# Nyström attention with a mixture of experts: quarter loads for the first batch, weight scales built from exponent bits, and a new order of work

## The chip, the cores and the metric

The kernel runs on one core of one Trainium2 chip. The metric is device time in microseconds of one execution, median of several runs; lower is better. The core has five engines that run in parallel, each in the order of its own instruction list: PE (TensorE, matrix products), DVE (VectorE), ACT (ScalarE), POOL (GpSimd) and SP (SyncE, which here only issues transfers). Sixteen DMA engines move data between HBM and the on-chip memory. An instruction waits on semaphores for what it needs, and everything behind it on its engine waits with it.

## The reference

The attention is Nyström's with 32 landmarks per head; its output goes through a mixture of eight experts, each token to the one expert of its highest gate. Shapes are 8 batches x 8 heads x 576 tokens x 64.

```python
m = 32; scale = 1/8
q_lm = q.reshape(B,H,m,18,D).mean(3);  k_lm = k.reshape(B,H,m,18,D).mean(3)
A, Bm, C = sm(q, k_lm), sm(q_lm, k_lm), sm(q_lm, k)      # softmax(scale * a @ b.T)
Z = Bm.T / (norm1(Bm) * norminf(Bm) + 1e-6)
for _ in range(6): Z = 2*Z - Z @ Bm @ Z
x = (A @ Z @ C @ v)                                       # 4608 tokens x 512
logits = xn @ en.T / tau;  e = argmax(logits);  gate = max(softmax(logits))
out[tokens of e] = gate * (relu(x @ w1[e]) @ w2[e])
```

## The kernel before, in words

Work is cut by batch: 576 tokens, all 8 heads, in eight batches. For each batch the attention part makes landmark sums of keys and queries (`sums`), inverts the 32x32 landmark matrix in six steps (`inverse`, `powers`), forms the weighted values (`values`, `weighted`), softmaxes the queries against the landmark keys (`queries`, `scored`: the tile `ab`), and joins the inverse and the weighted values to `wt` (`landmarks`). All tokens of a batch are guessed to go to one expert (`guess`, `choose`); the experts' weights for that guess are loaded (`weights`), and a last step (`mistakes`) counts tokens for which the guess was wrong and would start a general path.

The expert part runs in 16-bit pairs. `first_weights` multiplies the loaded w1 by `wt`, `scaled` writes the product as a high and a low half (`ww`) under a power-of-two scale, and `first` makes `ht = relu(ab @ ww)` from 96 matmuls of 288 columns. `second` makes the output from `ht` and `w2c`, which are scaled halves of w2. The scales come from three sums of squares or absolute values: `bound` (of `wt`), `first_scale` (of w1; for batch 0 one scale for each of its four quarters, "parts") and `second_weights` (of w2). Each sum is added across partitions by a one-column matmul in `total`; `scale_by` masks the exponent, and reciprocals turn it into a factor.

Loads are issued by SP alone, in order: keys and queries of batch 0 in two halves each, the values, batch 1's keys and queries, then weights as soon as a guess is there. `sums` takes each half either as one DVE reduction of 1152 elements a partition, or as an addition of halves on POOL (`half`) with a DVE reduction of 576.

The order is written out. Each step is a generator; the table TURNS names, turn by turn, the generator that goes on, CHOICES says which engine takes a step that several could take, BANKS which PSUM bank, and WARM at which turn how many dummy products of 128 columns PE gets (`keep_warm`, up to four in one matmul of up to 512 columns, line 604; nothing reads them). So the tables fix every engine's instruction list. Outputs leave through three `yt` tiles in turn; SP reads the count of wrong guesses (`misi`) into a register before the last outputs.

Lines that matter below: L648 loads, L682 and L685 sums, L1003 to L1018 `total` and `scale_by`, L1059 to L1066 `bound`, L1348 squares of w1, L1362 and L1364 its factor, L1416 and L1418 the two halves of `ww`, L514 every product, L1572 and L1574 the outputs.

## Time and profile before

| | before |
|---|---|
| median of 3 runs | 403.74 us (400.25, 403.74, 404.1) |
| the profiled execution, whole | 400.08 us |
| its span, first to last instruction | 398.4 us |
| mean granted TensorE clock | 0.998 |
| PE busy | 378.3 us (95%) |
| DVE busy | 317.9 us (80%) |
| ACT busy | 250.9 us (63%) |
| POOL busy | 91.0 us (23%) |
| moved by DMA | 78.78 MB |

The span is followed on one core. A busy engine is one with an instruction in flight, so a short wait that ends while the last product is still draining does not count as idle. The chain of waits goes back from the last instruction to whatever released each step, and so names the engine that set the end.

### The profile page before, as it was taken

How to read it: one execution, taken by the hardware profiler on the slowest of the kernel's cores; microseconds unless marked ns; L12 is line 12 of the kernel's file. 1: busy time of each engine (PE TensorE's matmuls, PEld its weight loads, DVE VectorE, ACT ScalarE, POOL GpSimd, SP SyncE). 2: the span in 40 equal slices, each digit the busy share in tenths (PEclk: the TensorE clock that was granted, in tenths of full speed). 3: DMA queues.
4: the chain of work that ended last, by engine and by line, in shares of the span. 5: the costliest groups of instructions: out<-in, count | busy, mean ns of one | idle time of the engine just before them, and what ended most of it. 6: DMA issues, size and time to landing. Idle time of an engine off the chain costs nothing.

```text
span 398.4 us, 15143 instructions
## 1 busy us (share of the span) xinstructions
PE 378.3 (95%) x6366; PEld 235.1 (59%) x6366; DVE 317.9 (80%) x921; ACT 250.9 (63%) x617; POOL 91.0 (23%) x94
## 2 busy tenths in 40 slices
PE   3789999999999999999999999999999999999993
PEld 1446745676645765567655675467745675478552
DVE  5999998899987989878997899658978886656521
ACT  1369986785688778735988793543786768336200
POOL 5164255301302131302455300102121220000100
PEclk9999999999999999999999999999999999999999
DMA  8997984517684997215993767015672085013012
GB/s 310 379 369 265 395 287 112 231 49 257 191 350 184 294 363 265 97 56 183 396 381 99 239 207 237 28 56 175 217 276 82 28 284 180 34 50 146 2 66 90
DMA packets 22669, 78.78 MB, mean 198 GB/s; under 512 B 2752, under 2 KB 5056, under 8 KB 20800
## 3 DMA queue, kind: packets, MB, share of 16 engines
q1 hardware_dynamic: 22304, 77.54, 54.0%
q8 instruction: 52, 0.85, 0.9%
q14 instruction: 25, 0.20, 0.2%
q10 hardware_dynamic: 288, 0.18, 0.2%
HBM read 62.96 MB, written 14.75 MB: 195 GB/s over the span
## 4 chain that ended last, share of the span: by engine, by line
PE 77%; DVE 11%; ACT 4%; DMA 3%; issue 2%; POOL 0%; SPq 0%; DVEq 0%; ACTq 0%
PE ps L514 75%; DMA wstage<-w 1%; DVE ht L1482 1%; ACT junk L1232 1%; DVE w2c L1472 1%; PE ps L604 1%; DVE cm L824 1%; DMA k_t<-kT 1%; ACT junk L1432 1%; DVE asum L961 1%; DMA out<-yt 1%; ACT ec L861 1%; ACT junk L1348 1%; DVE ww L1418 1%; DVE qsum L685 1%
## 5 line engine op out<-in xcount | busy, mean ns | idle before, releaser
L514 PE MATMUL ps<-w2c,ht 128*128 128x512 f16 (+2 forms) x1176 | 196.8, 340 | 0.0
L514 PEld LDWEIGHTS <-ht 128*128 128x128 f16 (+1 forms) x1176 | 95.2, 102 | 81.7 <-issue 3.2
L514 PE MATMUL ps<-ab,ww 128*128 128x288 f16 x768 | 101.0, 286 | 0.1
L514 PEld LDWEIGHTS <-ww 128*128 128x128 f16 x768 | 72.8, 98 | 24.2 <-issue 2.5
L1480 ACT ACTIVATE ht<-ps 128x288 f16<-128x288 f32 x128 | 48.2, 423 | 27.0 <-PE ps L514 26.3
L1482 DVE SCALAR_TENSOR_TENSOR ht<-ps,ht 128x288 f16<-128x288 f32 x128 | 53.7, 447 | 6.9 <-ACT ht L1480 6.6
L1232 ACT ACTIVATE junk<-ps 128x512 bf16<-128x512 f32 (+1 forms) x40 | 23.8, 595 | 29.0 <-DVE lga L1223 17.6
L1472 DVE SCALAR_TENSOR_TENSOR w2c<-wstage,wsc,w2c 128x1024 f16<-128x1024 f32 x28 | 37.0, 1322 | 2.1 <-ACT w2c L1470 2.0
L1348 ACT ACTIVATE junk<-wstage 128x1024 bf16<-128x1024 f32 x32 | 34.0, 1062 | 5.3 <-DMA wstage<-w 5.0
L972 POOL TENSOR_TENSOR ab<-at,ab 128x576 f16<-128x576 f32 x14 | 17.9, 1283 | 68.5 <-ACT ab L970 68.5
L1250 POOL TENSOR_TENSOR nrm<-ssq,half 128x5 f32<-128x5 f32 x8 | 9.4, 1175 | 97.4 <-ACT junk L1232 97.4
L1470 ACT ACTIVATE w2c<-wstage,wsc 128x1024 f16<-128x1024 f32 x23 | 26.1, 1148 | 4.8 <-PE ps L514 2.5
L1432 ACT ACTIVATE junk<-wstage 128x1024 bf16<-128x1024 f32 x25 | 26.5, 1059 | 2.1 <-DMA wstage<-w 1.7
L1574 ACT ACTIVATE yt<-ps,gfac 128x512 f32<-128x512 f32 (+1 forms) x26 | 15.8, 619 | 18.9 <-PE ps L514 17.8
L861 ACT ACTIVATE ec<-ps,cneg 128x144 f32<-128x144 f32 x64 | 23.4, 388 | 6.1 <-DVE cneg L851 3.5
L682 POOL TENSOR_TENSOR half<-q_t 128x576 f32<-128x576 f32 x13 | 17.9, 1380 | 27.4 <-DMA q_t<-qT 7.5
L1416 ACT ACTIVATE ww<-ps,wsc 128x1024 f16<-128x1024 f32 (+1 forms) x18 | 17.6, 1018 | 10.1 <-PE ps L514 3.6
L981 POOL TENSOR_TENSOR ae<-ae,am 128x576 f32<-128x576 f32 x13 | 17.1, 1315 | 26.9 <-DVE am L955 20.8
L1418 DVE SCALAR_TENSOR_TENSOR ww<-ps,wsc,ww 128x1024 f16<-128x1024 f32 (+1 forms) x18 | 20.6, 1156 | 0.7 <-ACT ww L1416 0.6
L682 POOL TENSOR_TENSOR half<-k_t 128x576 f32<-128x576 f32 x11 | 14.2, 1295 | 26.1 <-DMA k_t<-kT 20.4
L514 PE MATMUL ps<-ek 32*32 32x64 f32 (+1 forms) x768 | 16.0, 214 | 2.4 <-DVE ek L1035 2.1
L981 POOL TENSOR_TENSOR ae<-ae,asum 128x576 f32<-128x576 f32 x9 | 10.4, 1157 | 33.4 <-DVE asum L795 8.3
(220 smaller groups left out, 497.2 us busy)
## 6 DMA issues: line engine op xcount, KB each, us to landing
wstage<-w SPq DMA_DIRECT2D x64, 512.0 KB, 6.3
v<-v SPq DMA_DIRECT2D x16, 640.0 KB, 5.1
k_t<-kT SPq DMA_DIRECT2D x7, 1152.0 KB, 9.4
q_t<-qT SPq DMA_DIRECT2D x7, 1152.0 KB, 8.6
out<-yt SPq DMA_DIRECT2D x31, 256.0 KB, 2.3
abs__140<-ab SPq DMA_DIRECT2D x8, 576.0 KB, 5.4
k_t<-kT SPq DMA_DIRECT2D x2, 576.0 KB, 4.5
q_t<-qT SPq DMA_DIRECT2D x2, 576.0 KB, 6.5
```

The costliest lines, as they stand in the source:

```text
L514: pe.matmul(o, lhsT, rhs, start=start, stop=stop)
L682: pool.tensor_tensor(out=half, in0=sv[:, :, :, 0:9], in1=sv[:, :, :, 9:18], op=ALU.add)
L861: act.activation(ects[g][:, QS * x:QS * x + QS], pc[:, a, c], AF.Exp, bias=neg[:, 4 * g + 2 * a + c:4 * g + 2 * a + c + 1], scale=SCALE / ...
L981: pool.tensor_tensor(out=x, in0=x, in1=z, op=op)
L1232: act.activation(junk[lo:hi, 0:512].rearrange("p (j g x) -> p j g x", j=4, g=2), pfv[lo:hi, :, n, :, 0:D], AF.Square, scale=1.0 / ASCALE, ...
L1348: act.activation(junk, stage[1, b, q], AF.Square, accum_out=sq[:, q:q + 1])
L1418: vec.scalar_tensor_tensor(out=ww[:, 1], in0=pw, scalar=sc, in1=ww[:, 0], op0=ALU.mult, op1=ALU.subtract)
L1432: act.activation(junk, stage[2, b, q], AF.Abs, accum_out=sq[:, q:q + 1])
L1470: act.activation(w[:, 0], st, AF.Copy, scale=sc)
L1472: vec.scalar_tensor_tensor(out=w[:, 1], in0=st, scalar=sc, in1=w[:, 0], op0=ALU.mult, op1=ALU.subtract)
L1480: act.activation(ht[:, 0, r], ph[:, 0:HS], AF.Relu)
L1482: vec.scalar_tensor_tensor(out=ht[:, 1, r], in0=ph[:, 0:HS], scalar=0.0, in1=ht[:, 0, r], op0=ALU.max, op1=ALU.subtract)
```

## The change

Four things are edited, and the tables that fix the order are replaced as a whole.

The keys and queries of batch 0 are loaded in four quarters each, and `sums` reduces each quarter of 576 elements by itself; the new CHOICES give all eight to DVE. The scales are built by integer arithmetic on exponent bits: `root` masks them, and one subtraction from a constant (or from `kw`) gives the reciprocal power of two, where a multiplication and a reciprocal stood. The addition of 1e-30 on DVE ahead of each total is gone: squares now carry a bias tile `tiny` (1e-17) on ACT and write the sum as bf16, and the accumulators of w2's sums are filled with 1e-30 by POOL at the start. `second_weights` takes the reciprocal of its total as it is. WARM asks for 200 dummy products where it asked for 93.

```diff
-TURNS = ("06060633000b33060606003300340b36...        (2050 turns)
+TURNS = ("000606060607060633063333060b060b...
-WARM = {20: 36, 37: 2, 90: 18, 100: 3, 105: 7, 111: 13, 159: 10, 216: 4}
+WARM = {3: 40, 26: 58, 45: 20, 75: 24, 92: 1, 96: 10, 102: 1, 114: 25, 137: 13, 204: 8}
...
+    absw = cst.tile([P, B, 5], F32, name="absw")
+    pool.memset(absw, 1e-30)
+    tiny = cst.tile([P, 1], F32, name="tiny")
+    pool.memset(tiny, 1e-17)
+    part16 = cst.tile([P, P], BF16, name="part16")
+    pool.memset(part16, 2.0 ** -15)
...
-            parts = 1 if b else 2                      # loads
+            parts = 1 if b else 4
-        parts = 2                                      # sums
+        parts = 2 if b else 4
...
-    def total(sq, n):
+    def total(sq, by=ones16):
-        yield V(4)
-        s16 = wst.tile([P, 4], BF16, name="ws16", bufs=3)[:, 0:n]
-        vec.tensor_scalar(s16, sq, 1e-30, None, op0=ALU.add)
         pf, done = yield from take(T(10, 2, cols=4), 1)
-        mm(pf[:, 0:n], ones16, s16)
+        mm(pf[:, 0:1], by, sq)
...
+    def root(f2):
+        hb = wst.tile([P, 1], I32, name="whb", bufs=4)
+        vec.tensor_scalar(hb, f2.bitcast(I32), 1, EXP_MASK, op0=ALU.logical_shift_right, op1=ALU.bitwise_and)
...
-        vec.tensor_scalar(hbw[:, b:b + 1], f2.bitcast(I32), 1, EXP_MASK, ...)         # bound
-        vec.tensor_scalar(invw[:, b:b + 1], hbw[:, b:b + 1].bitcast(F32), 2.0 ** 58, ...)
-        vec.reciprocal(scw[:, b:b + 1], invw[:, b:b + 1])
+        vec.tensor_scalar(kw[:, b:b + 1], hb, -1.0, float(264 << 23), op0=ALU.mult, op1=ALU.add)
+        vec.tensor_scalar(scw[:, b:b + 1].bitcast(I32), hb, -1.0, float(196 << 23), ...)
+        vec.tensor_scalar(invw[:, b:b + 1], hb.bitcast(F32), 2.0 ** 58, ...)
...
-                act.activation(junk, stage[1, b, q], AF.Square, accum_out=sq[:, q:q + 1])     # first_scale
+                act.activation(junk, stage[1, b, q], AF.Square, bias=tiny, accum_out=sq[:, q:q + 1])
-            yield from scale_by(inv, f2, 2.0 ** 59, True)
-            vec.tensor_scalar(sc, hbw[:, b:b + 1].bitcast(F32), 2.0 ** 58, inv, ...)
-            vec.reciprocal(sc, sc)
+            hb = yield from root(f2)
+            vec.tensor_scalar(sc.bitcast(I32), hb, -1.0, kw[:, b:b + 1], op0=ALU.mult, op1=ALU.add)
...
-        yield from scale_by(inv2[:, b:b + 1], f2, 2.0 ** -14, False)                  # second_weights
-        vec.reciprocal(sc, inv2[:, b:b + 1])
+        vec.reciprocal(sc, f2)
-        vec.tensor_scalar(ginv[:, b:b + 1], inv2[:, b:b + 1], inv1[:, b:b + 1], 1.0 / ASCALE, ...)
-        vec.tensor_scalar(ginv[:, b:b + 1], ginv[:, b:b + 1], invw[:, b:b + 1], ...)
+        vec.tensor_scalar(ginv[:, b:b + 1], sc1[:, b:b + 1], sc, ASCALE, ...)
+        vec.reciprocal(ginv[:, b:b + 1], ginv[:, b:b + 1])
```

DVE's list from its first landmark sum on, in the kernel before (`ksum`, `qsum` are the sums, `half` is what POOL has added ahead, `es` belongs to the experts' norms):

```order
L685 TENSOR_REDUCE ksum<-half 128x64
L685 TENSOR_REDUCE ksum<-k_t 128x64
L616 TENSOR_REDUCE es<-ps 128x8
L685 TENSOR_REDUCE qsum<-q_t 128x64 x2
L621 TENSOR_SCALAR er<-er 128x8
L623 RECIPROCAL er<-er 128x8
```

The same place in the changed kernel:

```order
L689 TENSOR_REDUCE ksum<-k_t 128x32 x4
L689 TENSOR_REDUCE qsum<-q_t 128x32
L620 TENSOR_REDUCE es<-ps 128x8
L689 TENSOR_REDUCE qsum<-q_t 128x32 x3
L625 TENSOR_SCALAR er<-er 128x8
L718 TENSOR_REDUCE bm_222<-ps 128x2
```

Four reductions, the first of them behind POOL, have become eight that wait for loads alone; the rows after them are the same work.

DVE's list where one of batch 0's four w1 factors is made, before (`ws` is the added 1e-30, `whb` the masked exponent, `wsc` the factor, `at` and `ws_` are attention work):

```order
L1003 TENSOR_SCALAR ws_593<-wsq 128x1
L967 STREAM_TRANSPOSE at<-ae 128x576
L1014 TENSOR_SCALAR whb<-ps 128x1
L1064 TENSOR_SCALAR invw<-hbw 128x1
L1018 TENSOR_SCALAR inv1h<-whb 128x1
L723 TENSOR_REDUCE bs_625<-be 128x2
L1362 TENSOR_SCALAR wsc_624<-hbw,inv1h 128x1
L1364 RECIPROCAL wsc_624<-wsc_624 128x1
```

And in the changed kernel (`sc1h` is the factor):

```order
L634 RECIPROCAL con<-con 128x1
L971 STREAM_TRANSPOSE at<-ae 128x576
L1012 TENSOR_SCALAR whb<-ps 128x1
L1095 COPY ws__648<-ps 128x128
L1360 TENSOR_SCALAR sc1h<-whb,kw 128x1
L636 TENSOR_SCALAR con<-con 128x1
```

Five rows for a factor have become two. Between DVE's row L623 (L627 in the changed kernel) and its first `ww` row there were 84 rows and are 73.

DVE's last rows, before (`misi` is the count of wrong guesses, `misf` and `mis16` lead to it, `yt` is an output):

```order
L1572 TENSOR_SCALAR yt_7206<-ps_74,gfac_123 128x512
L1572 TENSOR_SCALAR yt_7208<-ps_74,gfac_123 128x256
L1614 CAST misi_145<-ps_74 128x1
L1562 TENSOR_LOAD misi_145
L1572 TENSOR_SCALAR yt_7249<-ps_74,gfac_123 128x256
L1572 TENSOR_SCALAR yt_7254<-ps_74,gfac_123 128x512
```

And in the changed kernel:

```order
L1602 TENSOR_REDUCE misf_7100<-gs_7086 128x1
L1605 CAST mis16_7111<-misf_7100 128x1
L1567 TENSOR_SCALAR yt_7121<-ps_74,gfac_129 128x512
L1567 TENSOR_SCALAR yt_7129<-ps_74,gfac_129 128x512
L1609 CAST misi_150<-ps_74 128x1
L1557 TENSOR_LOAD misi_150
```

The output of 512 columns that was DVE's last instruction now stands ahead of the count, and both halves of the very last output go to ACT. On PE the count's product moves from behind 18 to behind 6 of the last chunk's 48 products of 256 columns.

## Rows read from the trace of the kernel before

**Rows 1.** Busy time by stretch: PE, PEld, DVE, ACT, POOL, then PEclk, DMA share, GB/s.
```profile
0.00:35.00 35.00, 23.60 (x568) 13.28 (x568) 29.77 (x105) 16.32 (x41) 15.56 (x35) 1.00 0.95 358
10.00:35.00 25.00, 20.06 (x560) 11.74 (x558) 24.04 (x91) 15.04 (x40) 10.29 (x11) 1.00 1.00 377
35.00:390.00 355.00, 353.11 (x5787) 220.64 (x5786) 287.40 (x816) 234.09 (x576) 75.45 (x60) 1.00 0.52 184
```

**Rows 2.** The chain that ended last: start us, us, engine and what.
```profile
0.81 4.00 DMA k_t<-kT
...
92.41 0.29 DVE ek L1035
...
160.74 20.05 PE ps L514 x557
```

**Rows 3.** Timeline of the start: start us, us, what, [idle before <- releaser].
```profile
1.73 1.18 SPq L648 DMA_DIRECT2D q_t<-qT  x2
...
6.20 0.75 DVE L685 TENSOR_REDUCE ksum<-half 128x64 f32<-128x576 f32 x1 [2.50 <-POOL half L682]
...
7.08 3.89 PE L604 MATMUL ps<-ones 128*128 128x512 bf16 x9
...
8.26 2.60 DVE L685 TENSOR_REDUCE qsum<-q_t 128x64 f32<-128x1152 f32 x2
...
17.87 1.15 PE L604 MATMUL ps<-ones 128*128 128x512 bf16 x5
```

**Rows 4.** Loads of the first and second query half: KB, us to landing.
```profile
q_t<-qT SPq DMA_DIRECT2D x1, 576.0 KB, 6.0
q_t<-qT SPq DMA_DIRECT2D x1, 576.0 KB, 7.0
```

**Rows 5.** DVE groups from 10 to 36 us: count, busy us, mean ns, idle before.
```profile
L1018 DVE TENSOR_SCALAR inv1h<-whb 128x1 f32<-128x1 f32 x4 | 0.6, 148 | 0.0
L1364 DVE RECIPROCAL wsc<-wsc 128x1 f32<-128x1 f32 x4 | 0.6, 148 | 0.1
L1003 DVE TENSOR_SCALAR ws<-wsq 128x1 bf16<-128x1 f32 x4 | 0.6, 146 | 0.0
```

**Rows 6.** Timeline from 26 to 34 us, the way to the first expert product.
```profile
26.96 0.27 ACT L1087 COPY wt<-ps 128x128 f32<-128x128 f32 x1 [0.45 <-PE ps L514]
...
29.67 0.67 ACT L970 CAST ab<-at 128x576 f16<-128x576 f32 x1 [0.22 <-DVE at L967]
...
30.25 1.05 ACT L1348 ACTIVATE junk<-wstage 128x1024 bf16<-128x1024 f32 x1
...
31.33 1.84 ACT L1416 ACTIVATE ww<-ps,wsc 128x512 f16<-128x512 f32 x3
...
32.67 0.74 DVE L1418 SCALAR_TENSOR_TENSOR ww<-ps,wsc,ww 128x512 f16<-128x512 f32 x1
...
33.06 1.07 PE L514 MATMUL ps<-ab,ww 128*128 128x288 f16 x6
```

**Rows 7.** The page's costliest groups: two ACT passes over 1024 columns.
```profile
L1348 ACT ACTIVATE junk<-wstage 128x1024 bf16<-128x1024 f32 x32 | 34.0, 1062 | 5.3 <-DMA wstage<-w 5.0
L1470 ACT ACTIVATE w2c<-wstage,wsc 128x1024 f16<-128x1024 f32 x23 | 26.1, 1148 | 4.8 <-PE ps L514 2.5
```

**Rows 8.** Timeline: an undisturbed run of second expert products.
```profile
370.62 5.57 PE L514 MATMUL ps<-w2c,ht 128*128 128x512 f16 x25
```

**Rows 9.** PE groups by shape, whole span: all products of that shape.
```profile
L514 PE MATMUL ps<-w2c,ht 128*128 128x512 f16 x744 | 169.1, 379 | 0.0
```

**Rows 10.** Timeline of the end.
```profile
388.17 3.44 PE L514 MATMUL ps<-w2c,ht 128*128 128x256 f16 x30
...
389.18 3.96 SPq L1579 DMA_DIRECT2D out<-yt  x3
...
391.64 0.47 ACT L1574 ACTIVATE yt<-ps,gfac 128x256 f32<-128x256 f32 x1 [15.02 <-PE ps L514]
392.03 0.75 DVE L1572 TENSOR_SCALAR yt<-ps,gfac 128x512 f32<-128x512 f32 x1 [2.27 <-DMA out<-yt]
```

## The prediction

> **What bounds the kernel now.** I read busy time by stretch first, then the chain of waits, then the timeline of the start and of the end. The stretches show three parts [rows 1]. Up to 35 us PE is busy 23.6 us of 35, so 11.4 us of its time are lost; between 10 and 35 us DVE is busy 24.04 of 25 us, so here DVE's list sets the pace. From 35 to 390 us PE is busy 353.1 of 355 us: it is the bound, and only 1.9 us stand open to be seen. After the last product the output drains. The chain says the same: it starts with the first key load, leaves PE at about 92 us, runs over DVE, ACT and one weight load, and is back on PE for good at 160.74 us [rows 2]. The work that PE has to do is not changed by the diff, so I cost what happens before PE is saturated, what happens after its last product, and what can move in between.

> The sum is made against the profiled execution, 400.08 us: 398.4 of span and 1.68 around it. The runs shown scatter by 1% about a median that is 3.66 us above it: 400.25, 403.74 and 404.1. The mean of these three and the profiled one is 402.0, and I put the forecast for a median on that.

> **Landmark sums.** Before, POOL adds the halves of the first load, DVE waits for it until 6.20, and the last sum ends at 8.26 + 2.60 = 10.86 us [rows 3]. The loads are close behind: the first key half is issued at 0.81 and lands 4.00 later, at 4.8 [rows 2]; the first query half lands at 1.73 + 6.0 = 7.7, and the second, issued about half of the 1.18 us later, at about 2.3 + 7.0 = 9.3 [rows 3, 4]. In the changed kernel eight sums of 576 elements run on DVE, 0.75 each (the row of that shape [rows 3]), 6.0 us in all against 4.7. The last quarter lands at about 9.4, as the same bytes are on the way, and its sum ends at 10.2 to 10.3. Gain 0.55 us. Bounds: if the first quarter comes no sooner than the first half does now, 4.8 + 6.0 = 10.8, nothing gained; if DVE could follow the 9.3 at once, 10.05, 0.8 gained.

> **Scales.** On DVE's list between L623 and the first half of `ww` stand 11 rows fewer. Small rows last 0.146 to 0.148 us [rows 5], 1.6 us in all; started in each other's shadow they are worth less, about 0.1 each. I take 1.2 and keep 0.9 and 1.65. By DVE alone the first DVE row of `ww` then moves from 32.67 [rows 6] by 0.55 + 1.2 to 30.9.

> ACT gives a later time. `wt` moves up by the sums and one removed row, 0.7 us, from 26.96 to 26.3. Then come three squares, one cast and the first part of `ww`. From `wt` to the cast, with two squares, ACT takes 29.67 - 26.96 - 0.22 of waiting = 2.49; the third square with its accumulator takes 1.08 (30.25 to 31.33), the cast 0.58 to the next start, a part of `ww` a third of 1.84, 0.61 [rows 6]. New is the bias tile, an operand read per partition. Two passes over 1024 columns differ by one such operand, a scale, and by 1148 - 1062 = 86 ns [rows 7]; no row has a bias tile at this length. With it, 26.3 + 2.49 + 1.08 + 3 x 0.086 + 0.58 + 0.61 = 31.3, when DVE's row can start: 32.67 - 31.3 = 1.35 us sooner. [...] Over the other batches the bias costs ACT 35 x 0.086 = 3.0 us (28 squares of w1 and 7 short ones), while DVE loses six rows in each of seven batches, 6.1 us.

> I take 1.2 us for the start, a little under ACT's 1.35 because every hand-over between the engines must hold; the bounds are 0 and 1.75 (DVE's own limit). The dummies are priced at nothing while PE waits anyway: 11.4 us lost there are their cover [rows 1]. [...]

> **The end.** Now SP sends three outputs only after the count of wrong guesses is there, at 389.18; a tile comes free by that, and DVE writes the last output at 392.03 to 392.78, although PE's last product ends near 391.6 and ACT's copy at 392.11 [rows 10]. In the new list that output is written ahead of the count, and the last instruction is ACT's copy, so the last transfer leaves 392.78 - 392.11 = 0.67 us sooner. I take 0.6; bounds 0 and 0.7.

> **The middle.** It is laid anew and nothing in the diff shortens PE's work there. Visible are 1.9 us of gaps [rows 1]. Short ones hide in the busy time: undisturbed, a product of 512 columns takes 5.57 / 25 = 0.223 us, and 744 of them 165.8; they took 169.1, so 3.3 us are hidden in this shape [rows 8, 9]. DVE's 6.1 us less against ACT's 3.0 more make a small gain likelier than a loss. I take 0.4, and for the range a gain of 4 and a loss of 4.

> **The sum.** 1.2 + 0.6 + 0.4 = 2.2 us. For an execution like the profiled one: 400.08 - 2.2 = 397.9. For the median, on the mean of the four: 402.0 - 2.2 = 399.8.

> **Rivals.**
> A: the new order also closes the gaps of the middle. It would take most of the 1.9 visible and 3.3 hidden us, 4.5 in all: 402.0 - 1.8 - 4.5 = 395.7. For it speaks that the chain is off PE from 92 to 161 us, on the engines that lose work; against it that gaps of both sizes belong to work in a fixed order of dependence, which a new list can only shift.
> [...]
> C, slower: ACT's list puts squares of w1 ahead of exponentials and `ht` copies that DVE and PE wait for. ACT already waits 5.0 us for weights to land [rows 7], hidden now. If the waits come to stand on PE's path and double, 10 - 1.8 = 8.2 us are lost: 410.2. It decides from 5.8 us on, where the loss passes 1%. Against it: DMA share is 0.52 after 35 us [rows 1], so most weights land early.
> D, slower: each smaller load pays its start-up again. The first load took 4.0 us, while the next ones followed at about 1.55 us [rows 2 to 4], so 2.45 is start-up; four more loads would cost 9.8 us and give 402.0 + 9.8 - 1.0 = 410.8; it decides from 1.25 us a load on. [...] The rows differ: 576 KB halves in one queue land 1.55 us apart, 380 GB/s, so the start-up of one lies under the transfer of another.

> **How the numbers follow.** Forecast 0.50, A 0.25, B 0.12, C 0.10, D 0.03. About 1% is what a measurement of this kernel can tell from no change. A is faster by 1.5%; of the forecast's 0.50 I give 0.07 to that side, since the runs of before scatter by 1%: faster 0.32. The rest of the forecast and B are the same: 0.55. C and D: slower 0.13. The range goes from 395.0, below A, to 403.5, which holds B and the forecast made on the shown median (403.74 - 2.2 = 401.5) with a loss of 2 in the middle; the likeliest case alone has 397.5 to 402.

> **What would show it.** Right: DVE's last sum of batch 0 ends at 10.1 to 10.5; the first `ab,ww` product starts at 31.3 to 32.4 instead of 33.06; squares of w1 take 1.14 to 1.16 us; from the end of the last product to the end of the span pass 0.6 us less; PE's idle time from there to the last product is 1 to 2.5 us. Wrong: dummies that still last 0.43 after 7 us (B), quarters that land more than 1 us apart (D), ACT idle for weights with PE idle behind it (C), or a middle that is shorter by more than 2 us (A).

## The result, and the profile after

The changed kernel takes 407.13 us (median of 18 runs, 403.73 to 411.69); the kernel before, run beside it, 402.66 us (18 runs, 399.17 to 405.67). The ratio is 1.0107, with a 95% interval of 1.0077 to 1.0138: slower by 1.1%, where 399.8 us and a range of 395.0 to 403.5 were forecast. The kernel before has two groups of executions, near 400.5 us at a granted clock of 0.99 or more and near 404.5 us at 0.98, and its profile is from the first.

The profiled execution took 409.04 us, of it 407.3 us of span (before 400.08 and 398.4). So the two traces lie 9.0 us apart where the medians lie 4.5 apart: the account from the traces below is of these two executions. The first view is busy time by stretch, as in [rows 1] (PE, PEld, DVE, ACT, POOL, then PEclk, DMA share, GB/s), with three short stretches below it.

```profile
0.00:35.00 35.00, 26.77 (x501) 13.32 (x505) 26.32 (x81) 11.55 (x33) 11.26 (x35) 0.95 0.90 324
35.00:390.00 355.00, 349.39 (x5821) 217.69 (x5814) 289.76 (x787) 242.25 (x589) 76.29 (x58) 1.00 0.52 185
23.00:26.30 3.30, 0.03 (x1) 0.00 (x0) 1.80 (x3) 1.72 (x3) 1.72 (x3) 1.00 0.94 347
26.80:30.10 3.30, 3.30 (x33) 1.29 (x27) 0.89 (x3) 0.00 (x0) 0.00 (x0) 0.54 0.84 295
190.60:194.00 3.40, 3.40 (x43) 2.34 (x39) 2.47 (x5) 1.73 (x4) 0.04 (x1) 0.54 0.67 244
```

After 35 us PE now loses 5.6 us instead of 1.9. By 35 us it has run 501 products instead of 568, although it was busier. From 23.0 to 26.3 us it does nothing, and the other engines run dry behind it; then it runs at a granted clock of 0.54, as again from 190.6 us. What it waited for stands in the table of waits (us in total, times, longest):

```profile
PE ps L512 <- issue: 6.9, 3, 3.3
```

"issue" means that nothing in the profile held the engine back. No such row exists for PE's products in the trace of before. PE's timeline around the three pauses (start us, us, what, count, [idle before <- releaser]):

```profile
22.08 0.95 PE L512 MATMUL ps<-v,ct 128*32 128x64 f32 x51
26.32 1.00 PE L512 MATMUL ps<-v,ct 128*32 128x64 f32 x29 [3.29 <-issue]
27.26 2.79 PE L608 MATMUL ps<-ones 128*128 128x512 bf16 x7
...
177.37 0.60 PE L512 MATMUL ps<-w2c,ht 128*128 128x512 f16 x2
179.09 1.69 PE L512 MATMUL ps<-w2c,ht 128*128 128x512 f16 x7 [1.11 <-issue]
...
186.20 0.45 PE L512 MATMUL ps<-ek 32*32 32x32 f32 x30
189.10 0.22 PE L512 MATMUL ps<-ek 32*32 32x32 f32 x2 [2.46 <-issue]
...
219.79 0.16 PE L512 MATMUL ps<-wsqw,ones 128*128 128x1 bf16 x1 [0.75 <-ACT junk L1107]
```

Each of the three breaks a series of products in its middle (51 of 80, 2 of 9, 30 of 32): the operands of the next one are those of the last, so a wait for another engine's result does not explain them. One row of the page, in the list of DMA queues (packets, MB, share), points to what may:

```profile
q8 instruction: 52, 0.85, 0.9%
```

This queue carries 52 packets of 16,384 bytes. TensorE's records in the trace (products, weight loads and a few semaphore instructions) number 12,825, which is 50.1 x 256. That the queue carries TensorE's program, 256 instructions in a packet, is an estimate from these counts and from where the pauses stand. Counted from 0 in order of time, the first instruction behind each of the three pauses is number 705, 6337 and 6849: 22 x 256 and 2 x 256 apart, and every one leaves 193 on division by 256. This gives the theory, **T1**: TensorE runs out of fetched instructions. By it the next packet is asked for when it enters the present one, and if it gets through 256 instructions before the next packet is usable, it stands still. The experiments test this; one part, when a packet is asked for, needs a correction (the section on full queues).

**Where the time went.** PE's last product ended at 391.61 us before [rows 10] and ends at 398.02 + 4.75 = 402.77 now, 11.16 us later. The three pauses are 3.29 + 1.11 + 2.46 = 6.86 of it. The two stretches at the lower clock (0.54) cost 1.6 to 1.7 each (below), 3.3. The wait at 219.79 us is worth 0.9, by which the other executions of this program are ahead there. Sum 11.1. What follows the last product is shorter: 407.3 - 402.77 = 4.5 us instead of 6.8.

```profile
398.02 4.75 PE L512 MATMUL ps<-w2c,ht 128*128 128x256 f16 x42
402.85 0.47 ACT L1569 ACTIVATE yt<-ps,gfac 128x256 f32<-128x256 f32 x1 [2.20 <-PE ps L512]
403.36 0.36 ACTq L1574 DMA_DIRECT2D out<-yt  x1
```

Theories to tell apart: T1; **R1**, the 107 dummy units more, of which seven products stand on the path at 27.26 us; **R2**, quarter loads that come late; **R3**, ScalarE's longer squares; **R4**, the new order of the work itself.

### The profile page after: what moved, and what is told of

The parts are those of the page before. It is cut to its first block, busy times and chain, and to the rows that moved or that the text cites. A ratio compares the mean times of both kernels' runs of the same rounds, so it can differ in the third digit from the quotient of the medians.

```text
span 407.3 us, 15155 instructions
## 1 busy us (share of the span) xinstructions
PE 388.9 (95%) x6394; PEld 239.0 (59%) x6394; DVE 317.4 (78%) x869; ACT 255.4 (63%) x624; POOL 87.5 (21%) x92
## 4 chain that ended last, share of the span: by engine, by line
PE 82%; DVE 5%; issue 4%; DMA 3%; ACT 3%; SPq 1%; ACTq 0%; DVEq 0%
PE ps L512 81%; DMA wstage<-w 2%; ACT junk L1346 1%; DMA k_t<-kT 1%; PE ps L608 1%; DVE ht L1477 1%; DVE cm L828 1%; DVE w2c L1467 1%; DVE qsum L689 1%; ACT junk L1229 1%; ACT ab L974 0%; DVE ksum L689 0%; SPq L1328 0%; SPq L652 0%; ACT ww L1412 0%
## 5 line engine op out<-in xcount | busy, mean ns | idle before, releaser
L1346 ACT ACTIVATE junk<-wstage,tiny 128x1024 bf16<-128x1024 f32 x32 | 36.7, 1148 | 5.1 <-DMA wstage<-w 4.6
L1247 POOL TENSOR_TENSOR nrm<-ssq,half 128x5 f32<-128x5 f32 x8 | 11.0, 1372 | 106.4 <-ACT junk L1229 106.2
L1428 ACT ACTIVATE junk<-wstage 128x1024 bf16<-128x1024 f32 x26 | 27.5, 1058 | 3.1 <-DMA wstage<-w 2.9
L976 POOL TENSOR_TENSOR ab<-at,ab 128x576 f16<-128x576 f32 x10 | 13.2, 1328 | 54.3 <-ACT ab L974 54.3
L1465 ACT ACTIVATE w2c<-wstage,wsc 128x1024 f16<-128x1024 f32 x21 | 23.8, 1143 | 1.6 <-PE ps L512 1.6
L686 POOL TENSOR_TENSOR half<-q_t 128x576 f32<-128x576 f32 x13 | 19.4, 1492 | 18.6 <-DMA q_t<-qT 11.5
L1412 ACT ACTIVATE ww<-ps,sc 128x1024 f16<-128x1024 f32 x14 | 15.0, 1112 | 11.8 <-PE ps L512 11.8
L1414 DVE SCALAR_TENSOR_TENSOR ww<-ps,sc,ww 128x1024 f16<-128x1024 f32 x14 | 17.8, 1274 | 3.1 <-ACT ww L1412 2.9
L985 POOL TENSOR_TENSOR ae<-ae,am 128x576 f32<-128x576 f32 x13 | 15.0, 1163 | 23.3 <-DVE am L959 23.3
```

Source lines behind the costliest of these rows:

```text
L686: pool.tensor_tensor(out=half, in0=sv[:, :, :, 0:9], in1=sv[:, :, :, 9:18], op=ALU.add)
L985: pool.tensor_tensor(out=x, in0=x, in1=z, op=op)
L1346: act.activation(junk, stage[1, b, q], AF.Square, bias=tiny, accum_out=sq[:, q:q + 1])
L1414: vec.scalar_tensor_tensor(out=ww[:, 1], in0=pw, scalar=sc, in1=ww[:, 0], op0=ALU.mult, op1=ALU.subtract)
L1428: act.activation(junk, stage[2, b, q], AF.Abs, accum_out=sq[:, q:q + 1])
L1465: act.activation(w[:, 0], st, AF.Copy, scale=sc)
```

## Experiments: the boundaries moved by empty instructions

Empty instructions (NoOp) in TensorE's program leave data and order as they are and are put in to move where the packets' boundaries fall in the work. Here n of them stand at the front:

```diff
+    for i in range(n):
+        pe.nop(hint=f"pad{i}", nofuse=True)
     wv.run([int(TURNS[i:i + 2], 36) for i in range(0, len(TURNS), 2)], CHOICES, BANKS, keep_warm)
```

**24 in front of the changed kernel.**

> The changed kernel with 24 empty instructions put at the very front of TensorE's program; nothing else differs. Theory T1 (TensorE runs out of instructions: its program comes in packets of 16,384 bytes, 256 instructions, each asked for when TensorE enters the packet before it; the three stalls named 'issue' of 3.29, 1.11 and 2.46 us stand at TensorE's instructions 705, 6337 and 6849, which all leave 193 on division by 256): each boundary now falls 24 instructions earlier in the work, so the stalls at 23.0, 178.0 and 186.7 us shrink or go (about 1.5 us left near 18 to 23 us, about 1 us near 177), the clock does not fall at 26.8 us, and the time is 403 us, 402 to 405. Rival R4 (the order of the work itself costs it): the time of the changed kernel, 407 within 1 us. Rival R1 (the dummy products): 407 within 1 us.

Measured: 400.75 us (10 runs), 0.9948 of before (0.9906 to 0.9989), 6.4 us below the changed kernel. In the traced execution, its slowest at 404.02, pauses of 2.50 and 1.92 us are left, again at instructions 705 and 6849, which are now 24 instructions earlier in the work. R1 and R4 fall as explanations of the whole: order and dummies are the same.

**20.**

> The changed kernel with 20 empty instructions at the front of TensorE's program, a neighbour of the run with 24 that was the first to be faster than the kernel before. T1: boundaries 4 instructions from that run's; 401 us, 400 to 403, and faster than the kernel before by 0.2 to 0.8%. If 24 was luck: 405 or more.

Measured: 400.79 us (12 runs), 0.9952 (0.991 to 0.9994). Not luck. Its trace has one long pause left, 2.73 us at instruction 705.

**176 in front of the changed kernel, 128 in front of the kernel before.**

> The changed kernel with 176 empty instructions at the front of TensorE's program. T1: boundaries fall 176 instructions earlier (80 later); by the passing times of the instructions in the trace of the changed kernel no packet near 19 to 26 us is run through in under 5.4 us, and the run between 180 and 190 us is cut elsewhere: no stall over 1 us before 60 us, time 403 us, 401 to 405. R4 and R1: 407 within 1 us.

> The kernel before with 128 empty instructions at the front of TensorE's program; nothing else differs. T1: the kernel before has its boundaries where few packets are run through quickly; moved by 128 instructions, packets are entered at about 11, 65, 91, 94, 125, 167 and 268 us that the passing times of its trace put at 1.8 to 5.5 us each, so stalls named 'issue' of 0.5 to 3 us appear there, and the time is 408 us, 405 to 413. R4 (the new order costs it) and any theory without packets: 402.7 within 1 us.

Measured: 419.75 us, ratio 1.042 (1.0316 to 1.0523), and 412.0 us, 1.0213 (1.0102 to 1.0323). Both mix two things, because empty instructions at the front are not free. PE's first product starts at 13.72 us with 176 of them and at 10.23 with 128, so one cost 3.49 / 48 = 73 ns there. With 176 the kernel is 11.7 us late by 22 us and 10.8 at the end, so only 0.9 us came from the boundaries where 4 were expected: new pauses (1.07 us at 37, 2.33 at 97 and 1.85 at 194 us) replaced the old ones. With 128 the kernel before is 5.6 us late at 60 us and 12.0 at the end; the 6.4 us between came in steps, the largest, in the time of the kernel before, at 168 to 174 (2.0), near 270 (1.3) and near 300 us (1.7). Pauses named issue, which before did not have, appear there; the longest of the seven in its waits is the late start itself (its waits, then PE's timeline):

```profile
PE ps L514 <- issue: 15.3, 7, 10.2
```

```profile
10.23 0.65 PE L514 MATMUL ps<-e,ones 64*128 64x64 f32 x2 [10.23 <-issue]
```

The four pauses of 0.6 us or more behind the start stand at instructions 4033, 6337, 9921 and 10945, all 193 over a multiple of 256.

**24 in front of the kernel before.**

> The kernel before with 24 empty instructions at the front of TensorE's program (128 of them cost about 76 ns each before TensorE's first product, which hid part of what the boundaries did; 24 end before ones16 is there plus about 1 us). T1: by the passing times in the trace of before, packets entered at 24, 91 and 199 us are then run through in 5.0, 3.7 and 4.6 us while transfers hold the queues full: stalls of 1 to 2 us near 95 and 203 us that the kernel before does not have, nothing elsewhere; 405 us against about 402.7, 404 to 407. Theory without packets: 402.7 within 1 us.

Measured: 403.86 us (10 runs), 1.0042 (0.9999 to 1.0086), against 401.06 beside it. The median moved the way that was expected, but the interval does not exclude no change, and the traced execution, one of the fastest at 400.02, shows no pause. So the two stalls named in the expectation were not seen, and for T1 this one settles nothing. It is a control all the same: 24 empty instructions alone did not make that kernel faster.

**24 hidden in the changed kernel.**

```diff
+LATE = (766, 767, 791, 793, 796, 799, 803, 804, 805, 806, 819, 823)
...
         for turn, n in enumerate(turns):
+            if turn in LATE:
+                warm(-2)          # two empty instructions
```

> The changed kernel with 24 empty instructions in TensorE's program not at the front but two at a time between the wide products of 112.7 to 120 us. T1: everything up to 112 us is as in the changed kernel (stall at TensorE's instruction 705 near 23 us still there, 1.6 to 3.3 us), and from there on the boundaries fall as in the run with 24 at the front: the stall near 178 us goes, the one near 186 us shrinks by 0.3 to 0.6 us; time 1 to 3 us below the changed kernel, 404 to 406. If the empty instructions cost their 76 ns each there: 1.8 us of that is eaten by 120 us. Theories of order, dummies or loads at the start: 407 within 1 us, or 1.8 us more.

Measured: 400.92 us (10 runs), 0.9955 (0.9916 to 0.9994): 6.2 us below the changed kernel, more than expected. This is the cleanest of them. Up to 112 us TensorE's program is the same, and the pause at 705 is there (2.20 us). The 52 wide products among which the 24 stand run as one piece, 0.219 us each, so they cost nothing:

```profile
110.95 11.39 PE L516 MATMUL ps<-w2c,ht 128*128 128x512 f16 x52
```

From there I compared the start of each instruction with that of the same instruction in the changed kernel. The lead is constant between the boundaries and grows in steps: 1.8 us from 113 to 177, 3.1 at 181, 6.3 at 191, 7.5 at 196, 8.4 from 222 to the end. The steps at 181 to 196 are the two pauses that are gone, and the lower clock that followed the second: 7.45 - 3.33 = 4.12 us around a pause of 2.46, so 1.7 for the clock. From 35 us on PE idles almost as little as before:

```profile
35.00:390.00 355.00, 352.73 (x5779) 219.30 (x5778) 287.32 (x776) 240.30 (x585) 74.59 (x57) 1.00 0.53 186
```

Over all 17 traces, 34 pauses of 0.9 us or more are named issue after 14 us. The first product behind each is number 193 over a multiple of 256 or one of the next two (a weight load stands ahead of it).

The fetches settle what a pause ends with. Counted in order, fetch and boundary go together one to one, and behind each of the 34 pauses TensorE goes on 1.17 to 1.61 us after the end of the fetch of the packet that it enters. At none of the 836 boundaries of the 17 traces that have such a fetch does it enter a packet sooner than 1.17 us after that packet's fetch.

## Experiments: full queues

Between running the first instruction of a packet ("entered") and the first of the next one lie three times: until the next packet's fetch starts, the fetch, and until TensorE goes on. Worked out from the records of q8 and of TensorE (us):

```
kernel       instr.  entered  start after  fetch  goes on after  pause
before        6337   168.41     0.76       0.95       1.64        none
with 128      6337   174.20     0.76       1.15       1.45        1.13
changed       6337   175.63     1.16       0.95       1.34        1.11
changed        705    18.76     5.07       0.89       1.61        3.29
changed       6849   182.81     3.83       0.94       1.52        2.46
24 in front   6337   174.22    -1.06       0.96       2.42        none
```

With queues empty (the row "with 128": DMA share 0.02 from 172 to 178 us) the three make 3.36 us, with queues full (the two rows with 705 and 6849: 0.98 and 0.86 until the fetch starts) 7.6 and 6.3 us. The 34 pauses say the same. In the six with a DMA share of 0.00 between entering and fetch, the fetch starts after 0.75 to 1.17 us and the three make 3.3 to 3.7; in the other 28, with a share of 0.67 to 1.01, it starts after 1.4 to 5.1 us and they make 3.7 to 7.8. The least at any pause over 0.5 us is 2.94 us (0.86 us of pause, in the run with 176).

The last row is where T1 needs its correction. With 24 in front, the same dense run of small products passes 256 instructions in 2.32 us, 9 ns each, and there is no pause:

```profile
171.62 3.41 PE L512 MATMUL ps<-w2c,ht 128*128 128x512 f16 x15
174.96 0.65 PE L512 MATMUL ps<-ek 32*32 32x64 f32 x32
175.54 0.76 PE L512 MATMUL ps<-wgd,ab 32*128 32x72 f16 x72
176.24 0.65 PE L512 MATMUL ps<-ek 32*32 32x64 f32 x32
```

The packet was entered at 174.22, while the 15 wide products ran, but the fetch of its successor had begun at 173.16 and ended at 174.12. So a fetch can begin before the packet ahead of it starts to run; at 137 of the 836 boundaries it began more than 0.3 us earlier than that, up to 4.2. Why it began early there is not shown. In the changed kernel the boundary falls behind the wide products, 24 instructions later in the work: entered at 175.63, and the fetch began 1.16 us after. Here that is what the 24 change.

Most boundaries have no long pause: 34 of the 836 have one of 0.9 us or more. In a dense run there was one: in the changed kernel the 256 instructions ahead of 6337 were through 1.11 us before the next ran.

To see whether full queues cause the delay, the kernel before got one transfer more. (Both expectations place the fetches 0.31 us too late against TensorE: their 1.07 and 1.33 us are the 0.76 and 1.64 of the first row.)

```diff
+            if turn == 1204:
+                act.dma_start(extra[:, :, 0:1024], w2[0, 0:2])    # the second run: w2[0], 2 MB
```

> The kernel before with one transfer more: 1 MB of w2 copied to an unused place in device memory, issued by ScalarE near 167 us, where the trace of before has the queues empty (DMA share 0.0 from 165 to 174 us) and where the packet entered at 168.41 us is run through in 3.35 us, its successor arriving 1.33 us before its first product. T1 with the queues' part in it: the fetch that starts 1.07 us after it is asked for there starts 3 to 5 us after it, so a stall of 1.5 to 3.5 us appears at TensorE's instruction 6337 near 171 us, which no run of before has; time 2 to 5 us more, 404.5 to 408. If only the number of instructions counts and not the queues: no stall there, 402.5 within 1 us.

Measured: 404.26 us (10 runs), 1.0034 (0.9989 to 1.0078), and in the trace no pause. The transfer ran from 165.9 to 169.5 us and was over before the fetch (DMA share 0.00 from 170 us); the fetch started 0.8 us after the packet ahead of it was entered. The test missed its target, so it says nothing.

> As the run with 1 MB added to the kernel before, with 2 MB, so that the transfer that began at 165.9 us and ended near 169.5 us lasts until about 173 us, over the fetch that is asked for at 168.8 us. T1 with the queues' part: that fetch starts 3 us or more after it is asked for (1.07 us before), and a stall of 1.5 to 3.5 us stands at TensorE's instruction 6337 near 172 us; time 1.5 to 4 us more than before. If only the number of instructions counts: no stall there, within 1 us of before.

Measured: 408.07 us (4 runs), 1.014 (1.0054 to 1.0226). PE's timeline in the kernel before, then with the 2 MB, then the stretches:

```profile
171.58 0.76 PE L514 MATMUL ps<-wgd,ab 32*128 32x72 f16 x72
```

```profile
175.07 0.40 PE L516 MATMUL ps<-wgd,ab 32*128 32x72 f16 x25
178.09 0.91 PE L516 MATMUL ps<-wgd,ab 32*128 32x72 f16 x47 [2.62 <-issue]
```

```profile
172.00:174.00 2.00, 2.00 (x80) 1.34 (x70) 1.79 (x5) 0.00 (x0) 1.54 (x2) 1.00 1.03 367
...
176.00:178.00 2.00, 0.00 (x0) 0.00 (x0) 0.00 (x0) 0.00 (x0) 0.00 (x0) 0.88 0.00 0
...
177.90:184.60 6.70, 6.51 (x96) 4.06 (x97) 2.63 (x4) 2.65 (x8) 0.00 (x0) 0.52 0.21 81
```

The packet was entered at 171.90 us; its successor's fetch started 3.77 us later instead of 0.76. The pause is at instruction 6337, inside the 72 products that ran in one piece before. Two details: from 176 us on no engine works, and the fetch itself is over at 176.75, yet the pause lasts until 178.09; and the granted clock falls behind it (0.52 from 177.9 to 184.6 us). The execution was 3.5 us late ahead of the transfer (lower clock near 28 and 34 us: 16 `wstage,wt` products took 1.04 and 1.10 us from 27.18 and 28.68 instead of 0.67 and 0.66, the first six `ab,ww` 1.65 instead of 1.07) and 9.2 behind it: 5.7 us for a transfer that nothing waits for, more than the 1.5 to 4 expected: 2.62 of it are the pause, and 2.8 were lost right behind it at that clock.

## Experiments: the parts of the change

**The dummies at 27 us taken out** (R1).

```diff
-            pe.matmul(warmth[:, 0:k * P], ones16, ...)
+            if n == WARM[114]:
+                pe.nop(hint=f"a{i}", nofuse=True)
+                pe.nop(hint=f"b{i}", nofuse=True)
```

> The changed kernel with the seven dummy products of turn 114 (the ones at 27.3 us, 2.79 us long) replaced by 14 empty instructions at the same place, so that no packet boundary moves. R1 (the dummies on the path are what the change lost): 403 us or less, and the stall at 23 us is a detail. T1: the stall of some 3.3 us before 26.3 us stays, only the 2.7 us of dummies that stood behind it go, of which at most 2 us come through: 405.5 us, 404.5 to 407.

Measured: 407.98 us (4 runs), 1.0115 (1.003 to 1.02): no gain. The pauses are there (1.65, 1.07, 1.39 and 2.46 us). Behind the first the clock stayed low until 32.5 us instead of 29.9 (granted clock up to 35 us 0.90 instead of 0.95). R1 falls for these seven; the early dummies are all in the runs with 20 and 24, which are faster than the kernel before.

**Halves again** (R2).

```diff
+                if b:
                     sp.dma_start(dst[b][:, r], src[b][:, r])
+                elif i % 2 == 0:
+                    sp.dma_start(dst[b][:, i:i + 2], src[b][:, i:i + 2])
```

> The changed kernel with the first batch's keys and queries loaded in two halves each (as before), the sums still four pieces on VectorE. TensorE's program is the same, instruction for instruction. Rival R2 (the quarters came late, about 1.25 us apart, and SyncE spent 0.46 us on each issue, so the sums ended at 10.83 us and not at 10.1 to 10.5 us): the last sum ends 0.5 us earlier or more, v, k1 and q1 are issued about 1.8 us earlier, time 1 us less or more than that. T1: the start moves by under 0.5 us, the stall near 23 us stays or grows (transfers as dense as before), time 407 within 1 us.

Measured: 405.1 us (4 runs), 1.0103 (1.0033 to 1.0173), within the scatter of the changed kernel. DVE's last sum ends at 8.82 + 2.06 = 10.88 us against 10.83, although the last query load lands at 9.38 instead of 10.05: the first half lands later than the first quarter (4.67 against 3.89), and the eight sums start later. Pauses of 2.20, 0.92 and 2.18 us are there. R2 falls.

**No bias tile on the squares** (R3).

```diff
-                    act.activation(junk, stage[1, b, q], AF.Square, bias=tiny, accum_out=sq[:, q:q + 1])
+                    act.activation(junk, stage[1, b, q], AF.Square, accum_out=sq[:, q:q + 1])
```

> The changed kernel without the bias tile on ScalarE's squares (1e-17 is not added ahead of squaring; it only guards a scale against zero). Squares last 1.06 us instead of 1.15 us. Rival R3 (ScalarE's longer squares and the new order on it): first product ab,ww 0.3 us earlier or more and 1 us or more off the time. T1: ScalarE waits for the weights' loads ahead of most squares; time 407 within 1 us, stalls at TensorE's instructions 705 and 6849 as in the changed kernel.

Measured: 405.67 us (10 runs), 1.0087 (1.0048 to 1.0125): the change's loss is still there. Pauses of 1.65, 1.11, 0.56 and 2.18 us stand at instructions 705, 6337, 6593 and 6849. This execution did not lose the clock near 27 us (its seven dummies took 1.52 us there instead of 2.79), so it prices that: at instruction 790 it leads the changed kernel by 3.2 us more than at 662, with a pause 1.64 us shorter. 1.6 us are the clock.

**Longer scale chains.**

```diff
             vec.tensor_scalar(sc.bitcast(I32), hb, -1.0, kw[:, b:b + 1], op0=ALU.mult, op1=ALU.add)
+            back = wst.tile([P, 1], F32, name="back", bufs=4)
+            vec.reciprocal(back, sc)
+            vec.reciprocal(sc, back)
```

> The changed kernel with two reciprocals more (each the inverse of the other) behind the scale of each weight block and behind scw, so that these chains are about as long as in the kernel before. This gives the price of the exponent scales alone. As forecast, they save 0.3 us each at the four first blocks, so the first ab,ww product comes up to 1.2 us later and the time is 0.5 to 1.2 us more, 407.7 to 408.3. If they lay behind the squares' chain anyway: the first ab,ww product within 0.3 us, 407 within 1 us.

(The same two reciprocals stand behind `scw`.) Measured: 408.24 us (4 runs), 1.0101 (1.0002 to 1.0201). The interval holds the changed kernel and the forecast price alike. The start can be set beside that of the run with 24 hidden, whose TensorE program is the same up to 112 us: the two executions agree within 0.01 us from 23 to 31 us. Then the longer chains show. The first `ab,ww` product starts at 37.66 us against 35.06, 2.6 us later; 0.9 of it is one DVE instruction that took 1.11 us instead of 0.17. Ahead of it PE waits for DVE's `whb`:

```profile
36.15 0.66 PE L512 MATMUL ps<-ones,v 128*128 128x1 bf16 x20 [1.50 <-DVE whb L1012]
...
37.66 2.73 PE L512 MATMUL ps<-ab,ww 128*128 128x288 f16 x12
```

So in this pair the scale chains do lie on the way to the start, and for more than the 1.2 us forecast. What that is worth at the end stays open: a lower clock from 36.4 us on (12 `ab,ww` products took 2.73 us from 37.66 and 1.65 from 42.47) and other pauses lie over it.

## Experiments: a version without the pauses

Three attempts to place the boundaries by the packets' passing times. All missed.

```diff
+LATE = (246, 256, 272, ..., 1104, 1124, 1142)      # 64 turns, four empty instructions at each; 24 more at the front
```

> The changed kernel with empty instructions at four places: 24 at the front, and four at a time between wide products, 100 in 45 to 70 us, 48 in 112 to 120 us, 108 in 140 to 166 us, so that the boundaries fall 24, 124, 172 and 280 instructions earlier in the work. By the passing times in the trace of the changed kernel and fetches of 3.3 us with empty queues and 6.5 us with full ones, the packets that are run through too fast between 70 and 165 us fall from 6.9 us in all (24 at the front alone) to about 4. T1: 399.5 us, 398 to 401. If four at a time are not hidden (76 ns each): up to 19 us more, and the position of each place shows in the trace.

Measured: 403.54 us (4 runs), 1.005 (0.9972 to 1.0128). Four empty instructions at a time are hidden nearly as well as two: the lead over the changed kernel is the same at 45 and 70 us and at 140 and 166 us, and falls by 0.5 us over the place at 112 to 120 us. But the boundaries between 70 and 165 us were better at 24 than at my 124 and 172: the lead falls by 3.3 us from 82 to 125 us, with pauses of 1.09 and 0.98 us.

```diff
-WARM = {3: 40, 26: 58, 45: 20, 75: 24, 92: 1, 96: 10, 102: 1, 114: 25, 137: 13, 204: 8}
+WARM = {92: 1, 96: 10, 102: 1, 114: 25, 137: 13, 204: 8}
+LATE = (947, 949, 956, ..., 1098, 1101, 1103)      # 24 turns, four empty instructions at each
```

> The changed kernel without the dummy products of turns 3, 26, 45 and 75 (36 products, 72 instructions, all before 18 us), and with 96 empty instructions, four at a time, between wide products of 140 to 165 us, so that boundaries fall 72 instructions later before and 24 earlier behind. T1: the packet that runs dry at 23 us is now entered at about 20 us and lasts 5.5 us or more: that stall falls under 1 us; the clock rises later (10 to 16 us instead of 6.3 us), which costs under 1 us since TensorE waits there anyway; 399.5 us, 398 to 402. R1 in its other form (the early dummies are needed): 403 or more, lost before 20 us.

Measured: 405.54 us (4 runs), 1.0095 (1.0017 to 1.0173). The pause at 705 went: PE idles 1.16 us there, which the profile puts down to DVE. The kernel was 3.5 us ahead at 27 us. But without the early dummies the 32 products `q_t,ksum` from 15.48 us on took 684 ns each instead of 415, the granted clock was 0.52 from 30 to 40 us, where PE was busy all the time, and a pause of 2.83 us appeared at 87 us.

```profile
30.00:40.00 10.00, 10.00 (x161) 4.93 (x153) 8.07 (x30) 7.18 (x14) 3.72 (x3) 0.52 0.82 323
```

```diff
+FILL = {3: 7, 26: 3, 45: 2, 75: 2}                 # empty instructions behind each dummy of that turn
+LATE = (246, 256, 272, ..., 405, 411, 415)         # 23 turns, five empty instructions at each; 20 more at the front
```

> The changed kernel with all its dummies and 280 empty instructions: 20 at the front, 7, 3, 2 and 2 behind each dummy product of turns 3, 26, 45 and 75, 8 behind the last of turn 26 (165 by 18 us), and five at a time between wide products of 45 to 69 us (115 more). Boundaries fall 165 instructions earlier up to 45 us and 280, that is 24, from 70 us on. T1: the packet entered near 20 to 21 us is run through in 5.4 to 6 us, so the stall near 23 us falls under 1 us without the clock falling behind it, and the rest is as with 20 or 24 at the front: 398.5 us, 397 to 400.5. If it stays at 401 or above, the stall near 23 us is not worth what it measures, or the empty instructions among the dummies delay the start.

Measured: 405.96 us (12 runs), 1.0092 (1.0052 to 1.0132). The pause at 23 us is gone; two others took its place, and the clock fell behind both (six dummies took 2.19 us from 19.93 where the changed kernel's took 1.47; granted clock 0.50 from 32 to 42 us). By 14 us, ahead of both, the kernel was 3.8 us behind the changed one, so the empty instructions among the dummies did delay the start, as the expectation allowed.

```profile
17.66 0.59 PE L517 MATMUL ps<-ones,v 128*128 128x1 bf16 x17 [2.44 <-issue]
...
30.57 0.31 PE L517 MATMUL ps<-ek 32*32 32x64 f32 x6 [0.99 <-issue]
```

Before 35 us the queues are full (DMA share 0.90 in the changed kernel) and small products come dense; with the boundaries moved, two pauses of 2.44 and 0.99 us stood there in place of one of 3.29. The best versions stay those with 20 or 24 empty instructions, 400.8 to 400.9 us, 0.5% faster than the kernel before, by intervals that end just below 1 (0.9989 and 0.9994).

## Why the prediction was wrong

- **What was missing.** No term and no rival holds the packets. The step that failed is "The dummies are priced at nothing while PE waits anyway" and, with it, the middle as "laid anew". Time was counted in busy engines only; 36 dummy products ahead of 18 us and every product moved also shift where 50 boundaries fall, and at one of them a pause of 3.29 us and a fall of the granted clock to 0.54 were measured. In the profiled execution the pauses and the lower clock are 6.9 + 3.3 us. They are all of the sign: with order, dummies and work the same, 24 hidden empty instructions turn 1.1% slower into 0.5% faster. Whether the boundaries were moved to bad places by the dummies or by the new order is not separated by any run.
- **Sums: -0.55 forecast, none measured.** DVE started early, but the third and fourth key quarter came late, 1.25 us apart, and the last query quarter landed at 10.05 us, where the forecast had 9.4 "as the same bytes are on the way"; its sum ends 0.78 later:

```profile
3.92 1.51 DVE L689 TENSOR_REDUCE ksum<-k_t 128x32 f32<-128x576 f32 x2
5.94 0.75 DVE L689 TENSOR_REDUCE ksum<-k_t 128x32 f32<-128x576 f32 x1 [0.52 <-DMA k_t<-kT]
7.19 0.75 DVE L689 TENSOR_REDUCE ksum<-k_t 128x32 f32<-128x576 f32 x1 [0.50 <-DMA k_t<-kT]
...
8.71 2.12 DVE L689 TENSOR_REDUCE qsum<-q_t 128x32 f32<-128x576 f32 x3
```

  The end is 10.83 us against 10.86 [rows 3]. That is the text's lower bound by another road: it was for a first quarter no sooner than 4.8 us, and the first quarter landed at 3.89. The sign named for rival D (quarters over 1 us apart) came, its price did not: halves gave no other time.
- **Scales and ScalarE: 1.2 forecast for the start.** The bias tile was sized right, 1148 ns against the 1.14 to 1.16 us named. The first `ab,ww` product came at 37.81 us; less the pause and the clock, 32.8, so 0.3 us sooner than 33.06 [rows 6]. The run with 24 hidden, where the clock did not fall (mean 1.000), has 35.06 and a pause of 2.20, so 32.9; the run without the bias 34.02 and 1.65, so 32.4. The start brought 0.2 to 0.3 us of its 1.2, and 0.7 without the bias. The 1.2 was built on sums that end 0.55 us sooner, and they did not.
- **The end: 0.6 forecast, 2.3 measured.** From the last product to the end pass 4.5 us instead of 6.8, and 4.0 with 20 or 24 empty instructions. By the trace, the last transfer leaves 0.6 us after PE's last product instead of 1.2, which is the 0.67 that was named. It lands 2.2 us later instead of 2.7 (128 KB instead of 256), and from the landing to the end pass 1.7 us instead of 2.9: SP closes the program with 21 semaphore waits, which before all stand behind the last landing (396.08 to 397.44 us, landing at 395.49); now that ACT sends the last transfer, 8 of them are done ahead of it (403.66 to 404.54, landing at 405.56). No run tests this last part.
- **The middle: 0.4 forecast.** With the two pauses after 35 us hidden away, PE loses 355 - 352.73 = 2.3 us there, of it 1.09 in one pause left: about 0.7 less than before. With 20 in front, where no pause is left there, it is 1.3, so 0.6 less: of the right size. The one ScalarE wait of rival C's kind that reached PE is the 0.75 us at 219.79.
- **Dummies, and B of the chances.** Ten took 4.41 us from 1.73 (0.44 each) and the next fifteen 3.31 us from 6.43 (0.22 each). They end at 9.74 us, ahead of the last sum's 10.83. The 0.43 us named for B is 3.89 / 9 [rows 3]; the overshoot of the sums that B stands for in the chances and in the range is not in this trace.
- **The sum by luck.** Without pauses and lower clock PE's last product would end at 391.7 us by the sum above, at 391.1 by the run with 24 hidden (394.4 less 2.20 and 1.09) and at 390.8 by the run with 20 (395.3 less 2.73 and an estimated 1.7 for the clock), against 391.6 before: 0 to 0.8 us sooner, where start and middle were to bring 1.6. With the 2.3 of the end that is 2 to 3 us, where 2.2 were forecast from other terms. That this is what the change is worth is argued from three executions, and no run had all pauses gone; the nearest, at 398.15 us, is the fastest of the runs with 20.

Still open: why single executions of one program differ by 6 us and more. The pause at 705 alone measured 1.64 to 3.29 us in executions whose TensorE program is the same up to there, so late fetches have a part, but only one execution of each kernel was traced.

## What to carry to other kernels

Where an engine pauses in the middle of a series and the profile names nothing, count its instructions: pauses that stand a multiple of 256 apart were boundaries of its program's packets here. A new order, or a few products more, can then move the time for no reason of its own: here by 1.5% (24 hidden empty instructions, 6.2 us faster). A handful of empty instructions between wide products, where they are hidden, is a cheap test and can be the cure; where to put them was not foreseen here, as three planned versions missed. Dense runs of small products beside full DMA queues are where it hurt: 28 of the 34 pauses stood at a DMA share of 0.67 to 1.01. A planner should keep transfers away from them, or let the boundary ahead of such a run fall among wide products, where the next fetch began before the run did (173.16 against 174.96 us with 24 in front).
